# A fused attention and MLP kernel: the high halves of the first layer's weights are written by GpSimd, one copy per tile, instead of ScalarE

## The chip, the cores and the metric

The kernel runs on one core of a Trainium2 chip. The metric is the device time of one execution in microseconds (us); three runs gave 1169.42, 1169.66 and 1170.11, median 1169.66. One further execution was profiled, and all rows below are from it. Engines are called by the profile's names: PE is TensorE's matmul, DVE is VectorE, ACT is ScalarE, POOL is GpSimd, SP is SyncE, which here only issues DMAs.

## The reference

Causal linear attention with a decay per head, then a layer with `h * cos(h)`, then a gated layer with `silu(gate) * value`. Cut to what is computed:

```python
# q, k, v: (4, 8, 768, 64) f32
for t in range(S):
    state = gamma * state + einsum('bhd,bhe->bhde', k[:, :, t], v[:, :, t])
    y[:, :, t] = scale * einsum('bhd,bhde->bhe', q[:, :, t], state)
x = y as (3072, 512)
h = x @ w_in;  x = (h * cos(h)) @ w_out              # w_in (512, 2048), w_out (2048, 512)
g = x @ w_gate;  out = (silu(g) * (x @ w_val)) @ w_out2   # w_gate, w_val (512, 1536)
```

The inputs of the weights reach the kernel as float64 words (pairs of 32-bit words), and the kernel turns each into a sum of two fp32r numbers, a high and a low half, so that three matmuls (high x high, high x low, low x high) give one product of nearly fp32 precision.

## The kernel before, in words

The 3072 tokens are 24 chunks of 128 (`c`), four chunks to a block of 512 tokens (`j`, 6 blocks). The first layer's hidden width of 2048 is 16 tiles of 128 (`m`). A unit is one pair of block and tile, 96 in all: 12 matmuls of 128x512 make `h` (L460, `project`), ACT and DVE turn it into `g` (L503 to L524), and 12 matmuls (L546, `output1`) add `g` times the second weight into the accumulators `o`; the output of a unit is issued two units after its `h`. Units run in the order block 0 tiles 0 to 6, block 1 tiles 0 to 15, block 0 tiles 7 to 15, then blocks 2 to 5. Attention (`sc`, `y`, `u`, `st`: scores, outputs, state updates, states) is woven between units. The gated layer follows from about 600 us on and is not touched.

Each first-layer weight tile `W1[m]` (128 partitions x 1024 columns: 512 of `w_in`, 512 of `w_out`) is prepared once, on the chip, in seven steps that are methods of `Weight`:

- `size` (L145, L146): ACT writes the absolute value of one word into `f`, POOL clamps it (`TENSOR_SCALAR f<-f`). `f` has two buffers.
- `low` (L153): DVE shifts and masks `f` in place. `round` (L161): ACT writes 16 bits of the raw words, 2.6 us.
- `merge` (L169): DVE combines raw words and `f` into the final fp32 value in `f`; both inputs lie in SBUF.
- `hi` (L173 to L175): a copy of `f` into half 0 of the tile `w`, in fp32r; before the change by `split_hi` (L127, L128), which is an ACT activation with Copy.
- `lo` (L177, L131): DVE subtracts half 0 from `f` and writes half 1; both inputs lie in SBUF. From tile 7 on the tile is also written back to HBM.

`h` of the unit that uses a tile needs half 0 for its first eight matmuls and half 1 for the last four. The order of work is written out by hand: the kernel is under a manual schedule, so each engine runs its instructions strictly in the order of the program. The first two tiles are prepared in a list at the program's start ("sc0 m0 y0 ... k0 k1 k2 k3 q4 k4 low1 merge1 hi1 lo1"), where `k` and `q` are POOL's scalings of keys (L309) and queries (L317) and `m` DVE's decay of the scores (L358). Tiles 2 and on are prepared by `hidden1`: its argument `a` holds the tiles that do `size`, `round` and `low` in this unit, `b` those that do `merge`, `hi` and `lo`. So in a unit's program the clamp of one tile stands before the `hi` of the tile ahead of it. POOL's other work are the state scalings (L421, `st`). `split_hi` also serves the attention outputs `x` and six tiles `parts` of the second layer, which stay on ACT.

Below, hi0, lo0, merge0 and so on mean the step of tile 0, and k0, q4 the scaling of chunk 0's keys and chunk 4's queries.

Of the kernel before, what the change touches and what calls it, by code (L numbers as in the profile page):

```python
# [91 lines left out]
def fused(ctx: ExitStack, tc: tile.TileContext, qkv, w1, w2, consts, out):  # L92
    nc = tc.nc
# [33 lines left out]
    def split_hi(src, dst):  # L127
        nc.scalar.activation(out=dst[:, 0], in_=src, func=AF.Copy)  # L128
# [7 lines left out]
    class Weight:  # L136
# [35 lines left out]

        def hi(self):  # L173
            self.w = self.pool.tile([P, 2, 1024], F32R, tag=self.tag, name=self.tag)
            split_hi(self.f, self.w)  # L175

        def lo(self):  # L177
            split_lo(self.f, self.w)
# [916 lines left out]
```

## Time and profile before

| what | value |
|---|---|
| median of three runs | 1169.66 us (1169.42 to 1170.11) |
| profiled execution, its own time | 1169.62 us |
| span of its trace | 1167.8 us |
| PE matmul busy | 1151.4 us, 99% of the span |
| DVE busy | 661.2 us, 57% |
| ACT busy | 590.4 us, 51% |
| POOL busy | 107.5 us, 9% |
| mean granted PE clock | 0.998 |

The span is the time from the first to the last instruction in the trace; what lies around it is 1169.62 - 1167.8 = 1.8 us. The busy shares are means over stages with different limits, so a stage is read by itself: first where PE stands idle, then which instruction released it. A row of a timeline has the start in us from the span's start, the duration in us, the engine, line and operation, the tiles (output `<-` inputs), the shape, how many instructions were merged into the row, and in brackets the idle time before with what ended it. A row of the chain of waits has start, duration, and engine, tile and line.

### The profile page before, as it was taken

The numbers are of one execution on the slowest core, as the hardware profiler recorded it, in microseconds if no ns is written. First come the engines' busy times: TensorE is split into PE (matmuls) and PEld (weight loads), VectorE is DVE, ScalarE is ACT, GpSimd is POOL, SyncE is SP. The second block draws the span as 40 slices with busy tenths as digits, with TensorE's granted clock in tenths as the row PEclk, the third lists the DMA queues.
The fourth block names the chain that finished last, engine by engine and source line by source line (L and its number), as shares of the span: only waits on it lengthen the run. The fifth ranks groups of instructions, "written<-read, shape, count | busy, mean of one in ns | idle before, by whom it ended". The sixth has DMA issues, their size and how long they took to land.

```text
span 1167.8 us, 16311 instructions
## 1 busy us (share of the span) xinstructions
PE 1151.4 (99%) x6532; PEld 940.1 (81%) x6532; DVE 661.2 (57%) x1075; ACT 590.4 (51%) x871; POOL 107.5 (9%) x98
## 2 busy tenths in 40 slices
PE   8899999999999999999999999999999999999998
PEld 5688878888888888878888888878888888888886
DVE  6866765467676667675656545574444473444330
ACT  4958974457675767677755333342233242232220
POOL 3511221012111211010000000000000000000000
PEclk9999999999999999999999999999999999999999
DMA  9517843235886698499675456665457666547461
GB/s 358 210 37 253 330 153 112 73 132 204 312 340 231 249 350 310 150 369 337 225 304 232 176 194 264 226 250 238 185 201 290 220 244 257 198 152 280 166 249 36
DMA packets 54220, 265.57 MB, mean 227 GB/s; under 512 B 5760, under 2 KB 6016, under 8 KB 33152
## 3 DMA queue, kind: packets, MB, share of 16 engines
q1 hardware_dynamic: 54144, 264.53, 60.5%
q8 instruction: 51, 0.84, 0.3%
q14 instruction: 25, 0.20, 0.0%
HBM read 213.13 MB, written 51.38 MB: 226 GB/s over the span
## 4 chain that ended last, share of the span: by engine, by line
PE 90%; ACT 5%; DVE 2%; issue 0%; DVEq 0%
PE h L460 20%; PE o L546 20%; PE o L731 17%; PE X L680 16%; PE Z L680 8%; PE Y L680 4%; PE y L382 2%; ACT rw L161 2%; PE sc L341 1%; PE y L374 1%; ACT w L128 1%; ACT f L145 1%; PE y L405 1%; ACT g L523 0%; DVE f L169 0%
## 5 line engine op out<-in xcount | busy, mean ns | idle before, releaser
L731 PE MATMUL o<-wo,g 128*128 128x512 f32 x864 | 205.4, 389 | 0.0
L460 PE MATMUL h<-x,w 128*128 128x512 f32 x780 | 191.5, 394 | 2.7 <-DVE x L131 1.5
L731 PEld LDWEIGHTS o<-wo,g 128*128 128x128 f32 x864 | 162.2, 188 | 33.7
L546 PE MATMUL o<-g,w 128*128 128x512 f32 x780 | 187.7, 389 | 1.1 <-DVE x L131 1.1
L460 PEld LDWEIGHTS h<-x,w 128*128 128x128 f32 x780 | 144.1, 188 | 35.2 <-DVE x L131 1.6
L546 PEld LDWEIGHTS o<-g,w 128*128 128x128 f32 x780 | 146.2, 188 | 31.8 <-issue 1.5
L680 PE MATMUL X<-xo,wh 128*128 128x512 f32 x576 | 144.4, 389 | 0.0
L680 PEld LDWEIGHTS X<-xo,wh 128*128 128x128 f32 x576 | 108.0, 188 | 22.8 <-DVE xo L646 0.4
L711 ACT ACTIVATE g<-silu 128x512 fp32r<-128x512 f32 x72 | 45.6, 633 | 153.7 <-DVE silu L710 153.7
L503 ACT ACTIVATE n<-h 128x512 int32<-128x512 f32 x96 | 56.8, 592 | 73.9 <-PE h L460 73.4
L460 PE MATMUL h<-x,back 128*128 128x512 f32 x372 | 91.0, 393 | 0.0
L546 PE MATMUL o<-g,back 128*128 128x512 f32 x372 | 89.3, 389 | 0.0
L161 ACT ACTIVATE rw<-rw,above 128x1024 uint16<-128x1024 uint32 x34 | 89.1, 2621 | 0.0
L822 DVE TENSOR_TENSOR u<-Z,u 128x512 f32<-128x512 f32 x36 | 24.9, 691 | 112.9 <-PE Z L680 112.9
L546 PEld LDWEIGHTS o<-g,back 128*128 128x128 f32 x372 | 69.8, 188 | 14.5
L460 PEld LDWEIGHTS h<-x,back 128*128 128x128 f32 x372 | 68.9, 188 | 15.2 <-issue 0.5
L680 PE MATMUL Z<-xo,wh 128*128 128x512 f32 x288 | 73.2, 389 | 0.0
L680 PE MATMUL X<-x,wh 128*128 128x512 f32 x288 | 73.1, 389 | 0.0
L714 DVE TENSOR_TENSOR g<-silu,g 128x512 fp32r<-128x512 f32 x72 | 49.8, 692 | 37.4 <-ACT g L711 35.6
L680 PEld LDWEIGHTS Z<-xo,wh 128*128 128x128 f32 x288 | 54.0, 188 | 11.4 <-ACT p L810 0.2
L680 PEld LDWEIGHTS X<-x,wh 128*128 128x128 f32 x288 | 54.1, 188 | 11.2
L146 POOL TENSOR_SCALAR f<-f 128x1024 f32<-128x1024 f32 x34 | 39.7, 1169 | 247.5 <-ACT f L145 247.5
(668 smaller groups left out, 1438.4 us busy)
## 6 DMA issues: line engine op xcount, KB each, us to landing
wh<-w2d SPq DMA_DIRECT2D x36, 1024.0 KB, 7.5
wo<-w2d SPq DMA_DIRECT2D x36, 1024.0 KB, 6.5
rw<-in_w_dram SPq DMA_DIRECT2D x34, 1024.0 KB, 7.3
back<-w1d SPq DMA_DIRECT2D x31, 1024.0 KB, 6.9
wh<-w2d SPq DMA_DIRECT2D x36, 768.0 KB, 4.3
w2d<-parts SPq DMA_DIRECT2D x18, 1024.0 KB, 4.9
xo<-x2d SPq DMA_DIRECT2D x19, 512.0 KB, 7.4
w1d<-w SPq DMA_DIRECT2D x9, 1024.0 KB, 4.8
```

What stands on the lines that cost most here:

```text
L128: nc.scalar.activation(out=dst[:, 0], in_=src, func=AF.Copy)
L146: nc.gpsimd.tensor_scalar(out=self.f, in0=self.f, scalar1=LARGE, scalar2=SMALL, op0=ALU.min, op1=ALU.max)
L161: nc.scalar.activation(out=self.raw.bitcast(U16)[:, :, 2], in_=self.raw[:, :, 0].bitcast(U32), func=AF.Identity, scale=2.0**-29, bias=above,)
L382: nc.tensor.matmul(out=y[bank][D * half:D * half + D, slot, :], lhsT=kv[:, 1, h * D:(h + 1) * D], rhs=s_t[c][:, h % 2, h // 2, :], start=f ...
L460: nc.tensor.matmul(out=ps, lhsT=w[:, a, k * P:(k + 1) * P], rhs=x[:, b, k, :], start=n == 0, stop=n == len(order) - 1,)
L503: nc.scalar.activation(out=n, in_=h, func=AF.Identity, scale=TURN)
L546: nc.tensor.matmul(out=o_t[0][i], lhsT=w[:, a, i * P:(i + 1) * P], rhs=g[:, b, :], start=first and n == 0, stop=last and n == 2,)
L680: nc.tensor.matmul(out=ps, lhsT=w[:, a, k * P:(k + 1) * P], rhs=x[:, b, k, :], start=start and n == 0, stop=n == len(order) - 1, skip_grou ...
L711: nc.scalar.activation(out=g[:, 0], in_=s, func=AF.Copy)
L714: nc.vector.tensor_tensor(out=g[:, 1], in0=s, in1=g[:, 0].bitcast(F32), op=ALU.subtract)
L731: nc.tensor.matmul(out=o_t[0][i], lhsT=g[:, a, i * P:(i + 1) * P], rhs=w[:, b, :], start=m == 0 and n == 0, stop=m == M2 - 1 and n == 2,)
L822: nc.vector.tensor_tensor(out=u2, in0=Z, in1=u2, op=ALU.add)
```

## The change

One line of `Weight.hi`: the copy of `f` into half 0 of the tile is issued on POOL with `tensor_copy` instead of on ACT. It applies to the 16 tiles `W1`; the classes `Pair` and `Out` of the second layer have their own `hi`.

```diff
         def hi(self):
             self.w = self.pool.tile([P, 2, 1024], F32R, tag=self.tag, name=self.tag)
-            split_hi(self.f, self.w)
+            nc.gpsimd.tensor_copy(out=self.w[:, 0], in_=self.f)
```

ACT loses 16 instructions; POOL gets 16, each at the place in its own queue where the program has `hi`. PE, DVE and SP keep their order, with other waits.

POOL at the program's start, from the clamps of tiles 0 and 1 to the first state scalings: `CAST w_401` is hi0, `CAST w_460` hi1 and `CAST w_558` hi2; the lines `qkv` are k0 to k3, q4, k4, and `st` the scalings of the four states.

```order
-L146 TENSOR_SCALAR f<-f 128x1024 x2
+L146 TENSOR_SCALAR f<-f 128x1024
+L175 CAST w_401<-f 128x1024
+L146 TENSOR_SCALAR f<-f 128x1024
 L309 TENSOR_TENSOR qkv<-qkv,cst 128x512 x4
 L317 TENSOR_TENSOR qkv<-qkv,cst 128x512
 L309 TENSOR_TENSOR qkv<-qkv,cst 128x512
+L175 CAST w_460<-f 128x1024
 L146 TENSOR_SCALAR f<-f 128x1024 x2
 L421 TENSOR_TENSOR st_145<-st_145,cst 128x256
 L421 TENSOR_TENSOR st_146<-st_146,cst 128x256
 L421 TENSOR_TENSOR st_147<-st_147,cst 128x256
+L175 CAST w_558<-f 128x1024
 L421 TENSOR_TENSOR st_148<-st_148,cst 128x256
```

hi1 now stands behind six scalings of keys and queries and ahead of the clamps of tiles 2 and 3; hi2 stands behind three of the four state scalings.

DVE at the same place, with the engine or queue each instruction waits for in brackets: lo1 (`w_460`), which follows low1 and merge1.

```order
 L153 TENSOR_SCALAR f<-f 128x1024 [waits Pool_49]
 L169 SCALAR_TENSOR_TENSOR f<-rw_186,f 128x1024 [waits DMAHW3_49,DVE_49,Activation_49]
-L131 TENSOR_TENSOR w_460<-f,w_460 128x1024 [waits Activation_49]
+L131 TENSOR_TENSOR w_460<-f,w_460 128x1024 [waits Pool_49]
 L358 TENSOR_TENSOR s<-sc,cst 128x4x64 [waits PE_49]
 L358 TENSOR_TENSOR s<-sc,cst 64x2x64 x2
```

The order of DVE is what it was; lo1 waits for POOL where it waited for ACT.

POOL at the end of the preparation, units 17 to 21: `CAST w_1498` is hi13, `w_1581` hi14, `w_1623` hi15.

```order
+L175 CAST w_1456<-f 128x1024
+L175 CAST w_1498<-f 128x1024
+L146 TENSOR_SCALAR f<-f 128x1024 x2
+L175 CAST w_1581<-f 128x1024
+L175 CAST w_1623<-f 128x1024
 L317 TENSOR_TENSOR qk<-qk,cst 128x512
 L309 TENSOR_TENSOR kv<-kv,cst 128x512
```

hi14 stands behind the clamp of tile 15, which stood alone there before.

## Rows read from the trace of the kernel before

**Rows 1.** Page, part 1: busy time of each engine, share of the span, instructions.
```profile
PE 1151.4 (99%) x6532; PEld 940.1 (81%) x6532; DVE 661.2 (57%) x1075; ACT 590.4 (51%) x871; POOL 107.5 (9%) x98
```

**Rows 2.** Timeline of PE, first 60 us.
```profile
36.86 1.67 PE L341 MATMUL sc<-qkv 64*64 64x128 f32 x28 [4.36 <-DVE st L418]
...
46.26 1.63 PE L546 MATMUL o<-g,w 128*128 128x512 f32 x6 [1.07 <-DVE x L131]
```

**Rows 3.** Timeline of PE, 135 to 170 us.
```profile
145.22 3.02 PE L460 MATMUL h<-x,w 128*128 128x512 f32 x12 [0.38 <-DVE r__1450 L519]
...
157.24 3.02 PE L460 MATMUL h<-x,w 128*128 128x512 f32 x12 [0.84 <-ACT w L128]
```

**Rows 4.** Chain of waits, 15 to 50 us.
```profile
27.60 1.07 ACT w L128
...
28.69 2.10 DVE w L131
...
45.69 0.44 DVE x L131
```

**Rows 5.** Line 128: minimum/median/maximum ns of one, first and last start, shape.
```profile
L128 ACT ACTIVATE w<-f x16: 1042/1054/1063, 18.6 to 162.7; 128x1024 fp32r<-128x1024 f32 x16
```

**Rows 6.** Groups of ACT, 104 to 157 us: count, busy us, mean ns, idle before.
```profile
L128 ACT ACTIVATE w<-f 128x1024 fp32r<-128x1024 f32 x7 | 7.4, 1056 | 0.0
```

**Rows 7.** Timeline of POOL, first 200 us.
```profile
22.01 6.46 POOL L309 TENSOR_TENSOR qkv<-qkv,cst 128x512 f32<-128x512 f32 x4
28.43 1.28 POOL L317 TENSOR_TENSOR qkv<-qkv,cst 128x512 f32<-128x512 f32 x1
29.68 2.03 POOL L309 TENSOR_TENSOR qkv<-qkv,cst 128x512 f32<-128x512 f32 x1
31.67 1.04 POOL L146 TENSOR_SCALAR f<-f 128x1024 f32<-128x1024 f32 x1
35.71 1.66 POOL L146 TENSOR_SCALAR f<-f 128x1024 f32<-128x1024 f32 x1 [3.00 <-ACT f L145]
37.34 3.76 POOL L421 TENSOR_TENSOR st<-st,cst 128x256 f32<-128x256 f32 x4
...
71.68 1.03 POOL L309 TENSOR_TENSOR qkv<-qkv,cst 128x512 f32<-128x512 f32 x1
78.03 0.61 POOL L421 TENSOR_TENSOR st<-st,cst 128x256 f32<-128x256 f32 x1 [5.31 <-DVE st L420]
...
155.32 1.65 POOL L146 TENSOR_SCALAR f<-f 128x1024 f32<-128x1024 f32 x1 [4.58 <-ACT f L145]
```

**Rows 8.** Timeline of DVE, first 170 us.
```profile
35.25 1.22 DVE L169 SCALAR_TENSOR_TENSOR f<-rw,f 128x1024 int32<-128x1024 int32 x1
...
38.31 0.75 DVE L524 SCALAR_TENSOR_TENSOR g<-r__477,g 128x512 fp32r<-128x512 f32 x1
38.99 1.63 DVE L131 TENSOR_TENSOR w<-f,w 128x1024 fp32r<-128x1024 f32 x1
40.55 1.10 DVE L153 TENSOR_SCALAR f<-f 128x1024 int32<-128x1024 int32 x1
...
42.16 1.72 DVE L169 SCALAR_TENSOR_TENSOR f<-rw,f 128x1024 int32<-128x1024 int32 x1
...
47.56 1.22 DVE L131 TENSOR_TENSOR w<-f,w 128x1024 fp32r<-128x1024 f32 x1
48.69 0.69 DVE L153 TENSOR_SCALAR f<-f 128x1024 int32<-128x1024 int32 x1
...
154.85 1.22 DVE L169 SCALAR_TENSOR_TENSOR f<-rw,f 128x1024 int32<-128x1024 int32 x1
```

**Rows 9.** Timeline of ACT, first 100 us: the input of tile 2's clamp.
```profile
29.05 1.15 ACT L145 ACTIVATE f<-rw 128x1024 f32<-128x1024 f32 x1
```

**Rows 10.** Windows: length, busy us (instructions) by engine, granted clock, DMA share, GB/s.
```profile
36.00:38.00 2.00, 1.14 (x23) 1.10 (x26) 2.00 (x6) 2.00 (x4) 2.00 (x3) 0.67 1.03 428
38.00:40.00 2.00, 2.00 (x38) 1.67 (x34) 2.00 (x3) 2.00 (x2) 2.00 (x3) 0.50 1.01 404
```

## The prediction

> **What bounds the kernel now.** I read the busy times first [rows 1]: PE is busy for 1151.4 of 1167.8 us, so nothing that only shortens ACT's list can give back more than the idle 16.4 us, and anything that holds PE up once is carried to the end. So I looked for PE's idle times in its timeline. Behind the first 25 us there are four that matter: 4.36 us before 36.86, released by DVE's state copies, 1.07 us before 46.26, released by DVE's low half of `x` [rows 2], and, late in the preparation of the weights, 0.38 us before 145.22 and 0.84 us before 157.24 [rows 3]. Between 46.26 and 144 us PE's timeline has no bracket at all. Then I read the chain of waits over the first stage: from 27.6 to 46.1 us it runs over DVE with short turns through ACT, it begins with hi1 on ACT and lo1 on DVE, and it ends in the `x` row that releases PE at 46.26 [rows 4]. The part that matters is this: from lo1 to that `x` DVE works off its list in order with hardly a gap, so what delays lo1 delays PE at 46.26, and from there PE has nothing to make it up with except the two late idle times.
>
> **What the change removes.** Sixteen ACT copies of 1.05 us [rows 5]. At 157.24 PE waited for such a copy itself, and the idle at 145.22 came behind ACT too, through DVE's L519. Seven of them lie between 104 and 157 us, 7.4 us in all with no idle time before any [rows 6], far more than PE's two idle times of 0.38 + 0.84 = 1.22 us. So ACT's lag goes, and 1.22 us is the most that comes back. One new wait may take some of it: in the order hi14 stands behind the clamp of tile 15. In the trace of before that clamp starts at 155.32 inside merge14 (154.85 to 156.07) and takes 1.65 us, 0.61 more than the 1.04 of an undisturbed one [rows 7, 8]. Copied after it, hi14 is ready 0.9 + 1.04 = 1.9 us after merge14's end; ACT's copy was ready after 0.08 + 1.04 = 1.1. The steps ahead of it now come earlier, since ACT no longer lags, so I let this take between nothing and 0.6 us, 0.3 as my value. Gain: 1.22 - 0.3 = 0.9 us.
>
> **What a copy costs on POOL.** No copy of this size on POOL is in the trace. The nearest row is the clamp, one input and one output of 128x1024 fp32 on the same engine: 1.04 us undisturbed [rows 7]. From above I take the key scaling, which reads two inputs: 1.03 us for 512 columns, so 2.06 for 1024 [rows 7]. From below, DVE's one-input pass over 1024 columns at 0.69 us [rows 8]. I use 1.04, since the clamp has the same traffic.
> The Trainium skill, GPSIMD Engine Reference, section 3.1, has a tight loop at about 1.8 cycles per element at best; at its 1.2 GHz that makes 1024 x 1.8 / 1.2 = 1.54 us, an estimate from that page, and with it the sum below would be 2 x 0.5 = 1.0 us higher. The clamp's row, 1.04 us for two operations per element, contradicts it here, so it moves no term.
>
> **First stall: lo1 behind the key scalings.** hi0 lies in a free POOL and finishes long before lo0 needs it: no cost. hi1 needs merge1 (over just ahead of ACT's copy at 27.60) and, in its queue, k0 to k3 (22.01 to 28.43), q4 (to 29.7) and k4 [rows 4, 7]. k4 took 2.03 us beside lo1; with DVE now waiting it takes its undisturbed 1.03, so it ends at about 30.70 [rows 7]. hi1 runs from 30.70 to 31.74. lo1 therefore starts 31.76 - 28.69 = 3.07 us late. What follows on POOL is the clamp of tile 2, whose input ACT wrote until 30.2 before and, without hi1 ahead of it, now a microsecond earlier [rows 9]. Before, lo1 started during q4 and ran 2.10 us against the 1.22 of an undisturbed one, the first 1.0 of it held, and k4 then waited for it [rows 4 to 8]: whichever of two such instructions comes first holds the other up. If the clamp comes first, lo1 waits to 32.74 and ends 1.08 later (as it did after q4, from 29.71 to 30.79), at 33.82: 3.0 us late. If lo1 comes first it ends at 31.76 + 1.22 = 32.98, 2.2 us late. The clamp needs no signal from another engine, so I take 3.0.
> The Trainium skill, SBUF — State Buffer, section "Who interferes with whom", says the same of DVE instructions with two SBUF inputs: issue order decides, and the second fully blocks. By a proportional sharing of the port instead, lo1 would end nearer to the smaller delay; the trace's clamp at 35.71, 0.76 us from merge2's end (35.25 + 1.22) and 1.66 us long, is the rule's pattern [rows 7, 8].
> PE's `h` of unit 1 waits for hi1 too, but that takes nothing off its idle time before 36.86, because the state copies that release it are behind lo1 in DVE's list, and move by the whole delay [rows 2].
>
> **Second stall: lo2 behind the state scalings.** I tell times here as in the old trace, before adding the 3.0. hi2 on ACT did not hold lo2 up. On POOL it comes behind the clamp of tile 3 (ends 37.37) and three state scalings [rows 7]. Alone a scaling takes 0.61; the second and third meet `g` on DVE (L524 at 38.31, 0.75) [rows 7, 8], so the third ends at about 39.6 and hi2 at 40.6, where lo2 stood ready at 38.99. Then the fourth scaling goes first (to 41.15), and lo2 ends 1.08 later at 42.23 against 40.62: 1.6 late. Behind it q5 (1.28, as q4) now holds low3 to 43.5, so it ends at about 44.1 against 41.65, and k5 (1.03) holds merge3 to 45.1, which ends at about 46.15 against 43.88: 2.3 us late. If DVE comes first each time, lo2 runs before the fourth scaling (40.6 to 41.8), that one holds low3 to 42.3 and q5 merge3 to 44.1, which ends at 45.2: 1.3 late. I take 2.3. From hi3 on POOL has the copy ready before DVE reaches `lo` (k5, clamp and copy end at about 48.1 against lo3 at 47.56 + 2.3 = 49.9), so there is no third stall.
>
> **Sum.** The profiled execution took 1169.62 us, 0.04 below the median of the three runs: 1169.6 + 3.0 + 2.3 - 0.9 = **1174.0 us**.
>
> **Rivals.**
> - DVE first. Everything as above, but DVE's instruction gets in before POOL's next one: 1169.6 + 2.2 + 1.3 - 0.9 = 1172.2. For it: in the old trace lo1 did get in between q4 and k4. Against it: there lo1 was already waiting, here it waits for a signal from POOL.
> - A slow copy. At 2.06 us each of the two stalls grows by 1.02: 1176.0. Against it speaks the clamp's row.
> - A second spell at half clock. After the 4.36 us of idle PE's granted clock is 0.67 in 36 to 38 and 0.50 in 38 to 40 us, that is, it runs at 1.2 and not at 2.4 GHz for some 3.4 us (0.33 x 2 / 0.5 + 2 and a little) [rows 2, 10]. That spell is hidden, since DVE sets the time at 46.26. The idle before 46.26 grows from 1.07 to about 3.4 us; if the clock falls there too, it hits work that is on the path: half of 3.4, 1.7 us, 1175.7. Against it: it is still shorter than the 4.36.
> - Not slower: the collisions with POOL disappear. While DVE waits for hi1, POOL catches up, and DVE's later instructions meet an emptier POOL. Excess in the old trace over the undisturbed times: lo1 0.88, lo2 0.41, low3 0.41, merge3 0.50, together 2.2 us [rows 4, 8]. If all of it went and hi2 cost no wait, the first stall would be 3.07 - 2.2 = 0.9 us, and with 1.2 us back at 145 to 157 the time would be 1169.3. It decides at merge3: it holds if merge3 ends less than 1.2 us late. Against it: hi2 itself stands in the line of three scalings.
>
> **How the numbers follow.** Forecast 0.52, DVE first 0.20, slow copy 0.10, second spell 0.08, not slower 0.10. A change under 0.2%, 2.3 us, cannot be told from none, so slower begins at 1172.0. Of "DVE first" at 1172.2 I count a quarter (0.05) as the same; of "not slower" 0.06 as the same and 0.04 as faster, since more would have to vanish than I found; a little of the forecast's spread adds 0.02 to the same. Faster 0.04, same 0.13, slower 0.83. The range goes from 1171.4, a little under "DVE first" with the whole 1.22 us back (1171.9), to 1177.7, the slow copy with a second spell (1176.0 + 1.7).
>
> **What would show it.** In the changed trace: the copies on POOL at about 1.04 us; hi1 starting at about 30.7, when k4 ends, and k4 at 1.03 us; lo1 at about 31.8 with DVE idle for 4 us before it (or held to 32.7); PE's `sc` row at about 39.9 and its L546 row at about 51.6 instead of 46.26; DVE waiting for hi2 by 1.6 us; ACT with gaps between 105 and 160 us, and PE's idle there at 0.3 us. The prediction is wrong if hi1 starts before 29 us, if the `x` row before 46.26 moves less than lo1 does, or if PE gets new idle time after 60 us, for instance because a copy queued behind a clamp comes too late for `h`.

## The result and the profile after

The changed kernel takes 1176.31 us (median of four runs, 1175.73 to 1176.68) beside 1169.54 us for the kernel before on the same chip: ratio 1.006, 95% interval 1.0048 to 1.0072. That is 6.8 us slower where 4.4 were forecast; it lies in the forecast range and on the forecast side. The profiled execution took 1176.56 us with a span of 1174.5, which is 6.7 us more than the 1167.8 of before.

Part 1 of the page of the changed kernel shows what moved between the engines:

```profile
PE 1152.7 (98%) x6532; PEld 941.2 (80%) x6532; DVE 664.1 (57%) x1075; ACT 576.6 (49%) x855; POOL 125.0 (11%) x114
```

ACT lost 13.8 us and POOL gained 17.5 [rows 1]; PE is only 1.3 us longer busy, so most of the loss is PE standing idle. PE's timeline of the changed kernel, with the rows that answer to [rows 2, 3]:

```profile
32.11 3.28 PE L460 MATMUL h<-x,w 128*128 128x512 f32 x12 [2.13 <-POOL w L175]
40.21 1.67 PE L341 MATMUL sc<-qkv 64*64 64x128 f32 x28 [4.82 <-DVE st L418]
...
51.59 2.32 PE L546 MATMUL o<-g,w 128*128 128x512 f32 x6 [2.14 <-DVE x L131]
...
56.28 3.04 PE L460 MATMUL h<-x,w 128*128 128x512 f32 x12
...
163.95 3.02 PE L460 MATMUL h<-x,w 128*128 128x512 f32 x12 [1.37 <-POOL w L175]
```

Read it as a ledger. `sc` comes 40.21 - 36.86 = 3.35 us later than before, L546 51.59 - 46.26 = 5.33 later. The next `h` stands at 56.28; before it stood at 49.44:

```profile
49.44 3.02 PE L460 MATMUL h<-x,w 128*128 128x512 f32 x12
```

That is 6.84 later, so 1.5 us were lost between two rows with no idle time. From there to 146 us the rows of `h` are 6.84 to 6.86 us late, with no bracket. The last row is 163.95 - 157.24 = 6.71 late: the late stretch gave back 0.15 us where I had counted on 0.9. Behind it little changes, and 6.7 is the difference of the spans.

The brackets alone would say the opposite, 1.37 us of waiting after the change against 0.38 + 0.84 = 1.22 before. The starts of the rows settle it. Three units earlier `h` stood here, first before the change, then after it:

```profile
139.24 2.88 PE L460 MATMUL h<-x,w 128*128 128x512 f32 x12
```

```profile
146.10 2.88 PE L460 MATMUL h<-x,w 128*128 128x512 f32 x12
```

From there to the last row it is 157.24 - 139.24 = 18.00 us before and 163.95 - 146.10 = 17.85 after. Three units with no wait take 16.32 us (129.78 to 146.10 in the changed kernel). So the waits of before cost 1.68 us, more than their brackets, and the one of after 1.53.

POOL's timeline of the changed kernel (line 175 is the copy) shows the first two stalls being made:

```profile
22.37 6.46 POOL L309 TENSOR_TENSOR qkv<-qkv,cst 128x512 f32<-128x512 f32 x4
28.80 1.28 POOL L317 TENSOR_TENSOR qkv<-qkv,cst 128x512 f32<-128x512 f32 x1
30.04 1.04 POOL L309 TENSOR_TENSOR qkv<-qkv,cst 128x512 f32<-128x512 f32 x1
31.02 1.04 POOL L175 CAST w<-f 128x1024 fp32r<-128x1024 f32 x1
32.03 1.04 POOL L146 TENSOR_SCALAR f<-f 128x1024 f32<-128x1024 f32 x1
...
40.69 2.20 POOL L421 TENSOR_TENSOR st<-st,cst 128x256 f32<-128x256 f32 x3
42.84 1.03 POOL L175 CAST w<-f 128x1024 fp32r<-128x1024 f32 x1
43.83 0.61 POOL L421 TENSOR_TENSOR st<-st,cst 128x256 f32<-128x256 f32 x1
44.40 2.28 POOL L317 TENSOR_TENSOR qkv<-qkv,cst 128x512 f32<-128x512 f32 x1
```

The whole row of key scalings starts 0.36 us later than in [rows 7], because the raw words of tile 1 landed later in this execution; apart from that hi1 runs when k4 ends, k4 takes its undisturbed 1.04, and hi2 runs behind three state scalings. DVE's timeline shows what waits for these copies:

```profile
32.09 2.05 DVE L131 TENSOR_TENSOR w<-f,w 128x1024 fp32r<-128x1024 f32 x1 [4.16 <-POOL w L175]
...
43.90 1.62 DVE L131 TENSOR_TENSOR w<-f,w 128x1024 fp32r<-128x1024 f32 x1 [1.48 <-POOL w L175]
45.45 1.78 DVE L153 TENSOR_SCALAR f<-f 128x1024 int32<-128x1024 int32 x1
47.15 0.68 DVE L519 SCALAR_TENSOR_TENSOR r__546<-r__546,h 128x512 f32<-128x512 f32 x1
47.75 1.47 DVE L169 SCALAR_TENSOR_TENSOR f<-rw,f 128x1024 int32<-128x1024 int32 x1
```

lo1 starts 0.06 us behind POOL's clamp and takes 2.05 us, not 1.22: the clamp came first. low3 takes 1.78 us behind q5 (1.10 in [rows 8]).

PE's granted clock is the column behind the five busy times in the windows of the changed kernel:

```profile
42.00:44.00 2.00, 2.00 (x29) 1.67 (x22) 0.52 (x2) 1.52 (x3) 2.00 (x3) 0.50 0.91 369
...
52.00:54.00 2.00, 2.00 (x10) 1.10 (x12) 2.00 (x3) 1.26 (x2) 0.00 (x0) 0.56 0.03 8
54.00:56.00 2.00, 2.00 (x30) 1.67 (x32) 2.00 (x4) 0.04 (x1) 0.00 (x0) 0.58 0.00 0
```

Where before one spell at 1.2 GHz was hidden between 36.7 and 40.1 us [rows 10], there is now a longer one to about 45.4 us, also ahead of DVE's `x` and so hidden, and a second one behind the L546 row, where PE sets the time. This is the 1.5 us without idle time.

Last the late wait, in POOL's timeline and then in DVE's:

```profile
160.76 1.65 POOL L146 TENSOR_SCALAR f<-f 128x1024 f32<-128x1024 f32 x1 [5.15 <-ACT f L145]
162.35 1.54 POOL L175 CAST w<-f 128x1024 fp32r<-128x1024 f32 x1
```

```profile
160.28 1.22 DVE L169 SCALAR_TENSOR_TENSOR f<-rw,f 128x1024 int32<-128x1024 int32 x1
...
162.32 0.68 DVE L524 SCALAR_TENSOR_TENSOR g<-r__1535,g 128x512 fp32r<-128x512 f32 x1
```

The clamp of tile 15 is held by merge14 to 161.5, hi14 stands behind the clamp and is then held by L524, and ends at 163.89; PE's `h` follows at 163.95.

### The profile page after: what moved, and what is told of

Its sections match the earlier page's. It is cut to its first block, busy times and chain, and to the rows that moved or that the text cites. A ratio compares the mean times of both kernels' runs of the same rounds, so it can differ in the third digit from the quotient of the medians.

```text
span 1174.5 us, 16345 instructions
## 1 busy us (share of the span) xinstructions
PE 1152.7 (98%) x6532; PEld 941.2 (80%) x6532; DVE 664.1 (57%) x1075; ACT 576.6 (49%) x855; POOL 125.0 (11%) x114
## 4 chain that ended last, share of the span: by engine, by line
PE 85%; DVE 1%; ACT 0%; issue 0%; DVEq 0%
PE h L460 18%; PE o L546 18%; PE o L731 16%; PE X L680 16%; PE Z L680 8%; PE Y L680 4%; PE y L382 1%; PE sc L341 1%; PE y L374 1%; PE y L405 0%; DVE silu L710 0%; ACT g L711 0%; DVE xo L646 0%; DVE xs L636 0%; ACT x L642 0%
## 5 line engine op out<-in xcount | busy, mean ns | idle before, releaser
L546 PE MATMUL o<-g,w 128*128 128x512 f32 x780 | 188.4, 390 | 2.1 <-DVE x L131 2.1
L546 PEld LDWEIGHTS o<-g,w 128*128 128x128 f32 x780 | 146.5, 188 | 33.0 <-issue 2.5
L546 PE MATMUL o<-g,back 128*128 128x512 f32 x372 | 89.4, 389 | 0.0
L546 PEld LDWEIGHTS o<-g,back 128*128 128x128 f32 x372 | 69.8, 188 | 14.5
```

The costliest lines, as they stand in the source:

```text
L546: nc.tensor.matmul(out=o_t[0][i], lhsT=w[:, a, i * P:(i + 1) * P], rhs=g[:, b, :], start=first and n == 0, stop=last and n == 2,)
```

## The experiments

Each kernel is compared with the kernel before on its own chip (1169.2 to 1169.5 us). Lines shift by a few numbers where code was added, so I name rows by their work. The theory after the result: two stalls of DVE at the start (3.0 and 2.0 us), 1.5 us at half clock behind the second, and a late wait for hi14 that takes the place of the two late waits of before.

**Only the head back on ACT.**

```diff
-            nc.gpsimd.tensor_copy(out=self.w[:, 0], in_=self.f)
+            if W1.index(self) < 3:
+                split_hi(self.f, self.w)
+            else:
+                nc.gpsimd.tensor_copy(out=self.w[:, 0], in_=self.f)
```

> hi0, hi1 and hi2 go back to ACT, hi3 to hi15 stay on POOL. Theory (two stalls behind POOL's queue in the first 52 us and a spell at half clock behind the second, together 6.8 us, and nothing of note after): both stalls and the spell go; PE's L546 row that was at 51.6 us is back at about 46.3; the late wait for hi14 (1.37 us) stays in place of the 1.22 us of before, so 1169.5 + 0.15 = about 1169.7 us. Rival (the copies cost all through 60 to 165 us too, by blocking DVE's two-input instructions): 1171 us or more, with new idle time of PE between 60 and 160 us.

Measured 1169.27 us, ratio 0.9997 (0.9988 to 1.0006). PE's timeline:

```profile
46.07 1.63 PE L549 MATMUL o<-g,w 128*128 128x512 f32 x6 [0.71 <-DVE x L131]
156.65 3.02 PE L463 MATMUL h<-x,w 128*128 128x512 f32 x12 [1.11 <-POOL w L178]
```

These are its only brackets between 46 and 200 us. Thirteen copies on POOL cost nothing that can be measured, though they do hold up DVE's instructions now and then; the whole loss hangs on the first three.

**Only hi1 and hi2 on POOL.** The same edit with `W1.index(self) not in (1, 2)` as the condition for ACT.

> Only hi1 and hi2 are copied by POOL, the other 14 tiles by ACT. Theory: two of the sixteen copies make the whole loss of the start, 6.8 us; the late idle time stays as before the change (1.22 us, behind ACT), if anything a little different because ACT lags the same: 1169.5 + 6.8 = about 1176.3 us, with PE's second half-clock spell. Rival (the loss is spread over the sixteen copies): 1170 to 1172 us.

Measured 1175.8 us (1174.42 to 1177.33), ratio 1.0057 (1.0044 to 1.0069): two copies make nearly the whole loss. The runs scatter over 2.9 us, and the profiled one, 1174.42, is the fastest. PE's timeline and the windows behind it say why:

```profile
51.16 1.63 PE L549 MATMUL o<-g,w 128*128 128x512 f32 x6 [2.86 <-DVE x L131]
...
54.34 3.04 PE L463 MATMUL h<-x,w 128*128 128x512 f32 x12
```

```profile
52.00:54.00 2.00, 2.00 (x32) 1.42 (x32) 2.00 (x3) 1.43 (x3) 0.00 (x0) 1.00 0.03 8
```

L546 is released 4.90 us later than before the change, but in this execution the clock stayed at full, and the next `h` follows after 3.18 us, as in the kernel before (46.26 to 49.44); in the changed kernel it took 4.69. My expectation of a spell missed this execution. The other executions have no trace, but the mean granted clock of each is known: 0.997 at 1174.42 and 1174.93 us, 0.996 at 1175.8, 0.994 at 1175.97 and 1177.33. That fits a spell in the slower ones, and does not show where in the program it lay.

**PE kept busy in the wait.** Eight matmuls ahead of the first output of unit 0, into an accumulator that is started afresh behind them:

```diff
+FILL = 8
 ...
         w, g = weight1(m, 1), g_t.pop((1, j, m))
+        if j == 0 and m == 0:
+            wb = W1[0].w[:, 0].bitcast(mybir.dt.bfloat16)
+            for _ in range(FILL):
+                nc.tensor.matmul(
+                    out=o_t[0][0], lhsT=wb[:, :P], rhs=wb[:, :T], start=True, stop=True, skip_group_check=True
+                )
```

> The changed kernel with 8 extra matmuls of 128x512 in bf16 (about 1.75 us, into an accumulator that is then started afresh) ahead of the first output of unit 0, so that PE's idle time before the released L546 row falls from 2.14 to about 0.4 us; DVE's list is the same. Theory (the idle time there makes the granted clock fall, and this costs 1.5 us): no half clock at 52 to 56 us, L546 still released at about 51.6, time 1176.3 - 1.5 = about 1174.8 us. Rival (the second spell follows from the whole first 50 us, not from this idle time, or costs nothing): the spell stays and the time is 1176 us or more.

Measured 1174.45 us (1173.98 to 1174.88), ratio 1.0045 (1.0032 to 1.0059): 8 more matmuls, 1.9 us faster than the changed kernel, in all runs. PE's timeline and a window:

```profile
48.45 1.90 PE L548 MATMUL o<-w 128*128 128x512 bf16 x8
50.00 3.17 PE L553 MATMUL o<-g,w 128*128 128x512 f32 x12
```

```profile
52.00:54.00 2.00, 2.00 (x28) 1.34 (x28) 2.00 (x4) 1.27 (x2) 0.00 (x0) 1.00 0.04 8
```

There is no idle time left and no half clock. Of the 1.9 us, 1.5 is the spell: the next `h` stands at 54.72, in the changed kernel at 56.28. The `sc` row is 0.03 us off that of the changed kernel and the late wait 1.25 in place of 1.37, and a few tenths are scatter between executions. One reserve: in the run above, the clock stayed at full behind 2.86 us of idle PE, so one trace without a spell does not prove that the matmuls kept it away. The times speak for it: all five lie below all four of the changed kernel (highest 1174.88, lowest 1175.73).

**The stalls one by one.** The condition for POOL is `W1.index(self) == 1` in the first kernel, `== 2` in the second.

> Only hi1 is copied by POOL. Theory: the first stall alone, 3.0 us on DVE and on PE's L546 row (49.3 instead of 46.3), no longer idle time before L546 than before the change, so no second spell at half clock; late idle time as before: 1169.5 + 3.0 = about 1172.5 us. Rival (the two stalls are one: a late lo1 only costs because POOL then is late with hi2 as well): under 1171 us.

> Only hi2 is copied by POOL. Theory: the second stall alone, about 2.0 us on DVE between lo2 and x, PE's L546 at about 48.2; 1169.5 + 2.0 = about 1171.5 us, or 1.5 more in executions in which the clock falls behind the wait of about 3 us. Rival (hi2 is late only because the first stall lets POOL's list pile up): 1169.5 to 1170 us.

Only hi1: 1172.54 us (1172.11 to 1172.95), ratio 1.0031 (1.002 to 1.0043). Only hi2: 1172.62 us (1170.32 to 1173.42), ratio 1.0029 (1.0017 to 1.0041). PE's rows, first of hi1 alone, then of hi2 alone:

```profile
39.80 1.67 PE L344 MATMUL sc<-qkv 64*64 64x128 f32 x28 [4.82 <-DVE st L421]
...
49.20 1.63 PE L549 MATMUL o<-g,w 128*128 128x512 f32 x6 [0.54 <-DVE x L131]
```

```profile
48.13 2.66 PE L549 MATMUL o<-g,w 128*128 128x512 f32 x6 [2.32 <-DVE x L131]
50.72 1.13 PE L377 MATMUL y<-qkv,st 64*64 64x128 f32 x16
51.78 1.09 PE L385 MATMUL y<-s,qkv 128*64 128x128 f32 x16
52.81 3.02 PE L463 MATMUL h<-x,w 128*128 128x512 f32 x12
```

hi1 alone moves `sc` and L546 by 2.94 us each, hi2 alone moves L546 by 1.87; together 4.8, where the changed kernel has 5.33, of which 0.36 came from the late landing. So the stalls are two, and they add up. In the profiled execution of hi2 alone the clock fell behind the wait (0.60 in this window), and the next `h` came after 4.68 us instead of 3.18: the same 1.5 us again, which accounts for over 3 us lost to 2 us of stall in this execution; the other five have no trace.

```profile
48.00:50.00 2.00, 1.87 (x5) 1.55 (x6) 2.00 (x4) 1.97 (x3) 0.00 (x0) 0.60 0.03 8
```

**hi14 back on ACT as well.** The condition for ACT is `W1.index(self) in (0, 1, 2, 14)`.

> hi0, hi1, hi2 and hi14 on ACT, the other twelve on POOL. Theory: no stall at the start, and hi14 no longer stands behind the clamp of tile 15 on POOL while ACT has no lag any more, so PE has no idle time between 47 and 170 us: 1169.5 - 1.22 = about 1168.3 us, faster than both. Rival (hi14 is late because merge14 is late, whichever engine copies): an idle time of 0.5 to 1 us stays before the h at about 157 us, 1169 us or more.

Measured 1168.83 us, ratio 0.9996 (0.9988 to 1.0005): not to be told from the kernel before, nor surely from the run with only the head on ACT. PE no longer waits at 157 us; one wait came up behind it, where lo15 on DVE was late (it took 2.31 us beside POOL's scalings of queries and keys, not 1.22):

```profile
164.67 1.20 PE L463 MATMUL h<-x,w 128*128 128x512 f32 x4 [0.67 <-DVE w L131]
```

**hi ahead of the clamp.** Head on ACT; for the other tiles POOL does `hi` directly behind `merge`, and the next tile's clamp (a method of its own now) behind `hi`:

```diff
         each(b, "merge")
+        if early:
+            each(b, "hi")
+            each(a, "clamp")
         mid = late_mid + late_x
```

> hi0, hi1, hi2 on ACT, the other thirteen on POOL, and in their units hi stands directly behind merge and ahead of the next tile's clamp. Theory (PE's late wait of 1.1 to 1.4 us comes from hi14 standing behind the clamp of tile 15 and behind DVE's L524): hi14 starts with merge14's end, PE does not wait at 157 us, 1169.5 - 1.2 = about 1168.3 us. Rival (merge14 itself comes too late for either engine): an idle time of 0.5 us or more stays before that h, and the time is that of the run with hi0 to hi2 on ACT, about 1169.3 us.

Measured 1168.61 us (1167.45 to 1170.49), ratio 0.9994 (0.9985 to 1.0003). PE's rows:

```profile
157.47 2.11 PE L467 MATMUL h<-x,w 128*128 128x512 f32 x8 [0.23 <-POOL w L180]
160.00 1.20 PE L467 MATMUL h<-x,w 128*128 128x512 f32 x4 [0.41 <-DVE w L131]
```

Half of the wait went, half stayed: 0.23 + 0.41 = 0.64 us against 1.11. The two parts differ. The wait for hi14 itself is down to 0.23: it now runs right behind merge14 (from 156.38, merge14 ends at 156.25), which comes just in time. The 0.41 is new, a wait for lo14, which meets the clamp that was moved behind hi14 and takes 2.06 us instead of 1.22; POOL's row, then DVE's:

```profile
157.38 1.48 POOL L150 TENSOR_SCALAR f<-f 128x1024 f32<-128x1024 f32 x1
```

```profile
157.88 2.06 DVE L131 TENSOR_TENSOR w<-f,w 128x1024 fp32r<-128x1024 f32 x1
```

So most of the old wait was the order, little of it the rival's late merge14, and the new order has a price of its own. The profiled execution, 1170.49 us, is the slowest of the eleven; in it the raw words of tile 1 landed late (POOL's clamp of tile 1 starts at 22.51 us, before the change at 21.00), which moves L546 from 46.26 to 47.77.

**All on POOL, in a better order.** The same reordering for all sixteen tiles, with `hi1` ahead of `k3` in the list at the start and `q4`, `k4` behind the first unit's `h`:

```diff
-            "y3 xh3 xl3 sc4 round1 k0 k1 k2 k3 q4 k4 low1 merge1 hi1 lo1"
+            "y3 xh3 xl3 sc4 round1 k0 k1 k2 low1 merge1 hi1 k3 lo1"
```

> All sixteen copies on POOL as in the changed kernel, but POOL's queue is put in the order in which others need its results: hi1 ahead of k3, then k3, with q4 and k4 moved behind the first unit's h; in each unit hi directly behind merge and the clamp of the next tile behind it, both ahead of the state scalings. Theory (the loss is only POOL's order, nothing that the copies do by themselves): no stall of lo1, lo2 or h, lo1 at about 28.7 us, L546 released at 46.3 or a few tenths later, no idle time of PE between 47 and 170 us: 1169.5 - 1.2 = about 1168.3 us, at most 1169.3. Rival (POOL has no room at the start whatever the order: 1.04 us more in a queue that had no gap between 21.0 and 32.7 us delays some other result, a clamp or a key scaling, by as much): 1170.5 to 1172 us, with DVE's low2 or PE's u waiting for POOL instead.

Measured 1169.66 us, ratio 1.0007 (0.9999 to 1.0016): the loss is gone without a single copy going back to ACT, so it was POOL's order that cost it. The gain I expected did not come. PE's rows:

```profile
39.47 1.13 PE L378 MATMUL y<-qkv,st 64*64 64x128 f32 x16 [1.62 <-POOL st L425]
...
42.43 4.22 PE L464 MATMUL h<-x,w 128*128 128x512 f32 x12
...
50.93 3.02 PE L464 MATMUL h<-x,w 128*128 128x512 f32 x12
...
157.41 2.14 PE L464 MATMUL h<-x,w 128*128 128x512 f32 x8 [0.19 <-POOL w L179]
159.93 1.20 PE L464 MATMUL h<-x,w 128*128 128x512 f32 x4 [0.38 <-DVE w L131]
```

DVE is back in time (its `x` starts at 45.44, before at 45.69), but now the state scalings come later on POOL and `y` waits for them. The spell at 1.2 GHz, over at 40.1 us before the change, lasts to about 45 here, so the `h` at 42.43 takes 4.22 us, and no wait is left behind it to hide that in: the `h` at 50.93 is 1.49 us later than before (49.44). The late waits, 0.19 + 0.38 us, give only part of this back. How much of the 1.49 is the wait of `y` and how much the clock was not separated. The rival was right in kind: in a queue this full at the start, something else waits.

**The list a unit earlier.** If merge14 is just in time, the preparation can be moved: two halves in units 18 and 19, one in 20, none in 21. First with the copies as in the run with the head on ACT, then in the kernel before:

```diff
-... [0, 1, 1, 1, 2, 1, 1, 2, 2, 2, 1, 1, 2, 1]))
+... [0, 1, 1, 1, 2, 1, 1, 2, 2, 2, 2, 2, 1]))
```

> hi0, hi1 and hi2 on ACT, the other thirteen on POOL as in the changed kernel, and the last three halves of the preparation one unit earlier (two halves in units 18 and 19, one in 20, none in 21), so that merge14 and hi14 come a unit ahead of the h that needs them. Theory (what is left of PE's late wait comes from merge14 being just in time; ACT, without the copies, has room for the earlier round): no idle time of PE between 47 and 170 us, 1169.4 - 1.2 = about 1168.2 us, faster than both by 0.1%. Rival (six units with a round in a row are 5.6 us of ACT each against 5.4 us of PE, and the lag moves PE's wait to another unit): 1169 us or more, with ACT or DVE in the brackets of PE's rows.

> The kernel before the change, all copies on ACT, with the last three halves of the preparation one unit earlier. Theory (ACT has no room there: 6.6 us for a unit with both halves against PE's 5.4): ACT's lag grows and PE waits longer than 1.2 us in all, 1169.4 + 1 or more, about 1170.5 us. Rival (the late wait is a matter of the list alone, and POOL isn't needed for it): 1168.2 us as with the copies on POOL.

With the copies on POOL: 1167.69 us (1166.73 to 1168.21), ratio 0.9985 (0.9976 to 0.9994): 1.5 us below the kernel before, a small gain, but its interval leaves out 1. In the kernel before: 1170.45 us (1169.62 to 1171.7), ratio 1.0012 (1.0003 to 1.0021). The first has no bracket in PE's timeline between 46.09 and 200 us. In the second:

```profile
144.15 3.06 PE L460 MATMUL h<-x,w 128*128 128x512 f32 x12 [0.44 <-DVE r__1450 L519]
150.72 3.02 PE L460 MATMUL h<-x,w 128*128 128x512 f32 x12 [0.80 <-DVE r__1495 L519]
157.29 3.02 PE L460 MATMUL h<-x,w 128*128 128x512 f32 x12 [0.83 <-DVE r__1540 L519]
```

Three waits behind ACT's chain, 2.07 us in all where there were 1.22. So the change does free what ACT lacks in this stage; the freed time is only worth something once the list uses it.

## Why the prediction was right in sign and short in size

- First stall, lo1 behind the key scalings: 3.0 forecast, 3.35 - 0.36 = 2.99 measured; alone 2.94. hi1 starts at 31.02 (30.70 forecast, plus 0.36 for the late landing), with k4 at 1.04 us and the clamp ahead of lo1. This step held to a tenth.
- The copy's price: 1.03 to 1.04 us forecast from the clamp, and measured for eleven of the sixteen copies. The other five took 1.49 to 1.55, each behind a clamp and beside DVE's L524. The slow copy is out, though the time, 1176.3, lies nearest to its 1176.0: the rows decide between rivals, not the sum. By these rows the estimate of 1.54 us from the Trainium skill, GPSIMD Engine Reference, section 3.1, does not hold for this copy.
- Who comes first: POOL's next instruction, both times. The rival "DVE first" falls.
- Second stall, lo2 behind the state scalings: 2.3 forecast, 5.33 - 3.35 = 1.98 measured, 1.87 alone. q5 held low3 as forecast. Less the 3.35 us, lo2 ended at 42.17 (42.23 forecast), low3 at 43.88 (44.1) and merge3 at 45.87 (46.15), so the replay ran 0.28 us long in all. That L546 stands at 51.59 where 51.6 was forecast is luck: the late landing made up for this.
- The late gain: 0.9 forecast, 0.15 measured. This is the first mis-sized term. I let the new wait for hi14 take 0 to 0.6 us, 0.3 as my value, and its bracket has 1.37, as I counted only the clamp. hi14 ended 2.4 us behind merge14's end, not 1.9, for L524 held it after the clamp; before, ACT's copy ended 1.1 behind it. Without ACT's lag merge14 came 1.4 us earlier (160.28 against 154.85 + 6.85), and the later copy used up nearly all of that. This also is one of the forecast's signs of being wrong, new idle time of PE after 60 us behind a copy that is queued behind a clamp. What could come back was 1.68 us rather than the 1.22 of the brackets. Two runs bear it out: hi ahead of the clamp cuts the wait for hi14 to 0.23, and with the list a unit earlier no wait is left and the span, 1165.9 us, is 1.9 us below that of before, 0.2 of it from an earlier start.
- The second spell at half clock: I gave it 0.08 and left it out of the sum; it came, at 1.5 us (1.7 forecast). The argument against it, that the wait is shorter than 4.36 us, was no argument: waits of 2.14 and 2.32 us were followed by one. The run with PE kept busy shows the price; that the idle time is needed for the spell rests on its one trace and five times. What decides whether the clock falls behind such a wait stays open.

So in place of 3.0 + 2.3 - 0.9 = 4.4 the profiled execution has 0.36 + 2.99 + 1.98 + 1.51 - 0.15 = 6.7 us, the 0.36 being no effect of the change as far as the runs show: the clamp of tile 1, at 21.37 us here, starts at 20.81 with all sixteen copies on POOL in the better order and at 22.51 in a run with hi0 on ACT.

## What to carry to other kernels

An engine that is 9% busy over the span can still have a full queue where it matters: look up the stretch, and replay the queue in order, before giving it work. A copy moved off a loaded engine should stand in the new queue where its consumer needs it, and whatever now stands behind it is late too. Time freed on an engine that was late is only worth something when the work that waited for it is moved forward as well.

## What the runs showed of the hardware that I had not expected

The granted clock behind a wait is not fixed by the length of that wait: it fell to 1.2 GHz behind idle times of 2.14 and 2.32 us and stayed at 2.4 behind one of 2.86 us at the same place in the program. The spell cost 1.5 us each time. PE's wait for hi1 says the same: the clock stayed at full behind 2.13 us (changed kernel) and 2.53 us (only hi1), and fell behind 2.20 us (only hi1 and hi2) and 2.54 us (PE kept busy), where the `h` behind the wait took 4.27 and 4.61 us instead of 3.28. When a POOL instruction released a waiting DVE instruction with two inputs in SBUF, POOL's own next instruction still got in first, in the changed kernel by 0.06 us for lo1 (32.03 against 32.09), and the DVE instruction took 2.05 us instead of 1.22. The Trainium skill, SBUF — State Buffer, section "Who interferes with whom", states the blocking. That the releasing engine's next instruction wins is what these rows add.
